# A tuned DeltaNet and feed-forward kernel: the second feed-forward product as seven half-width block products from the third chunk on

## Chip, cores, metric

One core of a Trainium2 chip. The metric is device time in microseconds. The kernel before has a median of 737.25 us over four runs (736.81 to 739.62).

## The reference, cut to what matters

```python
# attention: per batch and head a delta-rule recurrence over 768 tokens, 4 batches, 8 heads of 48
# then x: (3072, 384), w_in: (384, 2048), w_out: (2048, 384), alpha: (2048,)
h = x @ w_in
g = np.maximum(h, 0.0) + alpha * np.minimum(h, 0.0)
return (g @ w_out).astype(np.float32)
```

All of it is fp32. The kernel cuts the sequence into 12 chunks of 64 tokens x 4 batches = 256 tokens each.

## The kernel before

A chunk's feed-forward is two products: `ffn_in` (L639) and `ffn_out` (L669). Python generators emit both in small parts and `weave` mixes them with the attention steps, so that TensorE always has feed-forward matmuls to do while attention waits for VectorE and ScalarE. An attention *step* is half a chunk; steps 4 to 23 are woven so. Each engine is given its instructions in the order in which the program emits them.

```python
def ffn_in(c):
    for f in range(0, FT, 2):                       # 8 groups of 2 row tiles
        p_h = ps_ffn().rearrange(...)               # one of two PSUM banks
        for i in range(2):
            for t in range(KT):                     # KT = 3
                nc.tensor.matmul(p_h[:, i], w_in[...], xt[:, t], ...)      # 128x256, L639
        nc.scalar.activation(low, p_h, ACT.Relu, scale=-1.0)
        for i in range(2):
            nc.vector.scalar_tensor_tensor(out=g[:, i], in0=low[:, i], ..., in1=p_h[:, i], ...)

def ffn_out(c, together=False):                     # order: bp = 0, 1; f = 0..15
    nc.tensor.matmul(p_o[bp], gs[f // 2][:, f % 2, bp * 128 : (bp + 1) * 128],
                     w_out[:, f], ...)              # 128x384, L669: 32 matmuls
    if f == FT - 1:
        nc.scalar.copy(o_sb, p_o[bp])
        ...                                         # two stores of 64 rows

for n in range(NJ, N):                              # NJ = 4, N = 24
    gens = [(attention(n), SHARES), (placing(n + 1, (1, 2)), SHARES * PLACING)]
    ...                                             # VectorE's block elimination, 3 steps of 4
    if n < NJ + 2:
        gens.append((part(late, ...), ...))         # second product of the second chunk
    else:
        gens.append((part(tail, (IN_PARTS + OUT_PARTS) // 2), ...))   # 40 parts a step
    weave(*gens)
```

## Time and profile before

| what | before |
|---|---|
| median time, span of the profiled run | 737.25 us, 733.0 us |
| TensorE busy | 706.1 us, 96% |
| VectorE busy | 400.3 us, 55% |
| one chunk's second product, nothing woven in | 20.66 us, 64 records |
| step 5 | 14.9 us, VectorE busy 95% of it |

Busy shares say what is full on average; the chain of waits says which engine sets the end; the table by stage says how much room the others have, and where. The lines are in the prediction. A "record" is one matmul instruction in the trace: a full fp32 matmul of this program leaves two of them.

### The profile page before, as it was taken

Reading aid. Unit: us, or ns where it says so; the run is one execution under the profiler, and the core shown is the slowest. Engines: PE = TensorE matmul, PEld = TensorE weight load, DVE = VectorE, ACT = ScalarE, POOL = GpSimd, SP = SyncE. Lnnn points to the kernel's source line nnn. Section 1 sums busy time; section 2 is a strip of 40 time slices with the busy share of each in tenths; the row PEclk is TensorE's granted clock in tenths of the full one; section 3 lists DMA queues with packets and bytes.
Section 4 is the critical chain, followed back from the end, with each engine's and each line's share of the span. In section 5 each row is a group of like instructions: output and inputs, shape, how many; then the busy total and the mean of one; then the engine's idle time right before and its main releaser. Section 6 shows DMA issues by size and latency. Waiting matters only on the chain.

```text
span 733.0 us, 20599 instructions
## 1 busy us (share of the span) xinstructions
PE 706.1 (96%) x8993; PEld 516.9 (71%) x8993; DVE 400.3 (55%) x1015; ACT 257.9 (35%) x606; POOL 18.1 (2%) x72
## 2 busy tenths in 40 slices
PE   6999978799999999999999999999999999999997
PEld 5457766556678678678678678678687687686774
DVE  6976889896886247655257565157464042141120
ACT  4625666505444144144134134134033132221110
POOL 3000001000000000000000000000000000000000
PEclk9999999999999999999999999999999999999999
DMA  8815863212322122122111201201211220100000
GB/s 146 205 30 139 193 167 95 74 22 45 58 56 45 24 45 45 26 42 45 30 39 34 45 14 33 45 15 33 44 21 25 44 39 7 34 2 2 23 1 21
DMA packets 110187, 37.63 MB, mean 51 GB/s; under 512 B 103392, under 2 KB 106480, under 8 KB 110096
## 3 DMA queue, kind: packets, MB, share of 16 engines
q1 hardware_dynamic: 108512, 36.01, 23.2%
q8 instruction: 71, 1.16, 0.7%
q10 hardware_dynamic: 1584, 0.30, 0.2%
q14 instruction: 20, 0.16, 0.1%
HBM read 31.56 MB, written 4.72 MB: 49 GB/s over the span
## 4 chain that ended last, share of the span: by engine, by line
PE 81%; DVE 11%; ACT 4%; issue 1%; DMA 1%; SPq 0%; DVEq 0%
PE p_ffn L669 33%; PE p_ffn L639 27%; PE p_ffn L737 5%; PE p_big L569 3%; PE p_big L341 2%; PE p_big L374 2%; DVE g L650 2%; PE p_big L596 2%; PE p_big L583 2%; PE p_big L526 2%; PE p_big L541 1%; PE p_big L612 1%; DVE prod L452 1%; DVE block L458 1%; DVE w_out L212 1%
## 5 line engine op out<-in xcount | busy, mean ns | idle before, releaser
L639 PE MATMUL p_ffn<-xt,w_in 128*128 128x256 f32 x1152 | 268.8, 386 | 9.8 <-DVE g L650 4.8
L669 PE MATMUL p_ffn<-w_out,g 128*128 128x384 f32 x768 | 258.8, 490 | 2.4 <-DVE g L650 2.4
L639 PEld LDWEIGHTS p_ffn<-xt,w_in 128*128 128x128 f32 x1152 | 213.2, 190 | 43.1 <-ACT w_out L200 6.8
L669 PEld LDWEIGHTS p_ffn<-w_out,g 128*128 128x128 f32 x768 | 142.6, 190 | 93.1 <-issue 2.9
L650 DVE SCALAR_TENSOR_TENSOR g<-low,al_t,p_ffn 128x256 f32<-128x256 f32 x192 | 83.5, 476 | 113.0 <-ACT low L647 111.9
L647 ACT ACTIVATE low<-p_ffn 128x512 f32<-128x512 f32 x96 | 57.2, 596 | 113.1 <-PE p_ffn L639 87.8
L675 ACT COPY o_sb<-p_ffn 128x384 f32<-128x384 f32 x24 | 11.5, 479 | 182.7 <-PE p_ffn L669 182.7
L458 DVE TENSOR_TENSOR block<-block,prod 128x30 f32<-128x30 f32 (+9 forms) x180 | 59.7, 332 | 6.2
L452 DVE TENSOR_TENSOR prod<-block 128x30 f32<-128x30 f32 (+9 forms) x180 | 58.9, 327 | 4.0
L572 DVE TENSOR_TENSOR r<-v_raw,p_big 128x384 f32<-128x384 f32 x22 | 12.0, 551 | 79.6 <-PE p_big L569 79.6
L737 PE MATMUL p_ffn<-k_t,ident 128*128 128x512 f32 x82 | 38.0, 611 | 0.0
L603 DVE TENSOR_TENSOR y<-y,p_big 128x384 f32<-128x384 f32 x22 | 12.1, 548 | 40.5 <-PE p_big L596 40.5
L418 ACT COPY same<-right 32x256 f32<-32x256 f32 x40 | 16.1, 403 | 49.4 <-DVE right L383 49.1
L737 PEld LDWEIGHTS p_ffn<-k_t,ident 128*128 128x128 f32 x82 | 15.3, 195 | 16.6 <-issue 16.2
L492 ACT ACTIVATE diag<-inverse,which 64x128 f32<-64x128 f32 (+2 forms) x62 | 25.3, 411 | 1.0
L577 ACT COPY y<-p_big 128x384 f32<-128x384 f32 x22 | 10.5, 480 | 35.5 <-DVE r L572 35.5
L363 ACT COPY k_t<-p_big 128x512 f32<-128x512 f32 x24 | 13.9, 581 | 24.3 <-PE p_big L341 24.2
L328 DVE RECIPROCAL rec<-norm 128x8 f32<-128x8 f32 x24 | 4.8, 200 | 31.2 <-ACT norm L326 31.1
L596 PEld LDWEIGHTS p_big<-u,a_t 64*64 64x64 f32 x768 | 13.4, 134 | 11.2 <-issue 8.2
L492 ACT ACTIVATE inv<-inverse,which 128x256 f32<-128x256 f32 x43 | 20.6, 502 | 0.5
L363 ACT COPY q_t<-p_big 128x512 f32<-128x512 f32 x24 | 14.0, 588 | 16.5 <-PE p_big L341 16.5
L392 DVE TENSOR_TENSOR a_t<-p_big,minus 128x256 f32<-128x256 f32 x48 | 17.8, 415 | 3.2 <-PE p_big L374 3.2
(97 smaller groups left out, 638.7 us busy)
## 6 DMA issues: line engine op xcount, KB each, us to landing
w_out<-in_moe_w_in_dram SPq DMA_DIRECT2D x12, 512.0 KB, 5.5
qp<-in_q_dram SPq DMA_DIRECT2D x48, 96.0 KB, 3.0
v_raw<-in_v_dram SPq DMA_DIRECT2D x48, 96.0 KB, 2.9
kl<-in_k_dram SPq DMA_DIRECT2D x96, 48.0 KB, 2.4
out_dram<-o_sb SPq DMA_DIRECT2D x48, 96.0 KB, 2.2
space_out<-in_moe_w_out_dram SPq DMA_DIRECT2D x11, 384.0 KB, 4.4
ke<-in_k_dram SPq DMA_DIRECT2D x43, 96.0 KB, 3.5
w_out<-in_moe_w_out_dram SPq DMA_DIRECT2D x5, 384.0 KB, 3.3
```

The lines of the kernel that those rows point to most:

```text
L363: nc.scalar.copy(dst.rearrange("p g i -> p (g i)"), src)
L392: nc.vector.tensor_tensor(out=a_t[n_q][:, a * G : (a + 1) * G], in0=p[:, a, 1], in1=minus[:, None, :].to_broadcast([128, G, C]), op=ALU.mult,)
L452: nc.vector.tensor_tensor(out=prod, in0=r[:, 0:j, j : j + 1].to_broadcast([128, j, n]), in1=r[:, j : j + 1, j + 1 : HB].to_broadcast([128, ...
L458: nc.vector.tensor_tensor(out=r[:, 0:j, j + 1 : HB], in0=r[:, 0:j, j + 1 : HB], in1=prod, op=ALU.add)
L492: nc.scalar.mul(dst[n % NE][to or rows, a.start * G : a.stop * G, cols], src[m][rows, heads], which[rows, i : i + 1],)
L569: nc.tensor.matmul(p[half(t), a, w, g], x[n][dims(a), g, half(t)], state[bp][dims(a), t, g])
L596: nc.tensor.matmul(p[half(t), a, g], a_t[n][half(t ^ a), a * G + g], us[n][half(t ^ a), a, g])
L639: nc.tensor.matmul(p_h[:, i], w_in[:, t, (f + i) * 128 : (f + i + 1) * 128], xt[:, t], start=(t == 0), stop=(t == KT - 1),)
L647: nc.scalar.activation(low, p_h, ACT.Relu, scale=-1.0)
L650: nc.vector.scalar_tensor_tensor(out=g[:, i], in0=low[:, i], scalar=al_t[:, f + i : f + i + 1], in1=p_h[:, i], op0=ALU.mult, op1=ALU.add,)
L669: nc.tensor.matmul(p_o[bp], gs[f // 2][:, f % 2, bp * 128 : (bp + 1) * 128], w_out[:, f], start=(f == 0), stop=(f == FT - 1),)
L737: nc.tensor.matmul(p, ident, k_t[NJ - 1].rearrange("p g i -> p (g i)"))
```

## The change

The second product is a 2x2 block product: token halves by column halves, contracted over even and odd row tiles. Strassen's scheme (in the variant with fifteen sums) makes it of seven block products instead of eight. The intent is to take an eighth off the arithmetic of the largest term of TensorE's chain (L669, 33%) and to give the sums to VectorE, which had 45% of its time free. The core of the diff, cut:

```diff
+    def operand_sums(b):
+        for dst, x, y, op in (
+            (s1, a21, a22, ALU.add), (s2, s1, a11, ALU.subtract), (a21, a11, a21, ALU.subtract),
+            (s4, a12, s2, ALU.subtract),
+        ):
+            nc.vector.tensor_tensor(out=dst, in0=x, in1=y, op=op)      # 128x512
+            yield
+    def weight_sums(b, first, last):                # 128x768, four for each half b, once
...
     def ffn_in(c):
+                    if (i, t) == (0, KT - 1):
+                        next(later, None)           # at most one sum in each later group
+            if c >= FAST and f == FT // 2 - 2:
+                later = operand_sums(0)
...
+    def ffn_out_fast(c):
+        later = operand_sums(1)
+        def product(x, w):
+            p = ps_ffn()[:, 0 : DM // 2]
+            for i in range(FP):                     # 8 matmuls of 192 columns
+                nc.tensor.matmul(p, x(i), w(i), start=(i == 0), stop=(i == FP - 1))
+                if i % 2 == 1:
+                    next(later, None)
...
+        p = yield from product(operand(0, 0), weight(0, 0))
+        nc.scalar.copy(u[0], p)
+        p = yield from product(operand(1, 0), weight(1, 0))
+        add(o[0][:, left], u[0], p)
+        p = yield from product(sum_(1), w_sum_(1))  # the first that reads a sum
+        add(u[0], u[0], p)
...                                                 # four more products, adds on VectorE
-            gens.append((part(tail, (IN_PARTS + OUT_PARTS) // 2), (IN_PARTS + OUT_PARTS) // 2))
+            parts = IN_PARTS - 4 if n % 2 == 0 else FAST_PARTS + 4
+            gens.append((part(tail, parts), parts))
+        if n == NJ + 1:
+            gens.append((weight_sums(0, 0, 3), 3))
+        elif n == NJ + 2:
+            gens.append((chain(weight_sums(1, 0, 3), weight_sums(0, 3, 4)), 4))
+        elif n == NJ + 3:
+            gens.append((weight_sums(1, 3, 4), 1))
```

Besides: the activation is written in place, into one buffer for all chunks but the second (whose activation goes where the sums will be), the two PSUM banks are fixed by name, tokens are regrouped so that a chunk's halves are contiguous, and each half is stored in four pieces of 32 rows instead of two of 64.

More of the change, by code (lines that the diff above doesn't have):

```diff
@@ L78, in ps_one @@
         return ps_big()[:, 0]
+    ffn_banks = [psum.tile([128, 512], FP32, name=f"p_ffn{i}") for i in range(2)]
+    turn = [0]
     def ps_ffn():
-        return psum.tile([128, 512], FP32, name="p_ffn", tag="ffn", bufs=2)
+        turn[0] ^= 1
+        return ffn_banks[turn[0]]
     def half(i):
@@ L621, in to_ffn @@
             xts[c] = work.tile([128, KT, TOK], FP32, name="xt", tag="xt", bufs=NXT)
-        p = ps_one()[:, 0:DM].rearrange("p (t i) -> p t i", t=KT)
+        p = ps_one()[:, 0:DM]
         y = ys[n].rearrange("p h d -> p (h d)")
         for t in range(KT):
-            nc.tensor.transpose(p[:, t], y[:, t * 128 : (t + 1) * 128], ident)
-        nc.scalar.copy(xts[c][:, :, bp * 128 : (bp + 1) * 128], p)
-    gss = {}
+            nc.tensor.transpose(p[:, t * 128 : (t + 1) * 128], y[:, t * 128 : (t + 1) * 128], ident)
@@ new lines, in to_ffn, with act_of @@
+        nc.scalar.copy(
+            xts[c].rearrange("p k (u b t i) -> p b k u t i", u=2, b=NB, t=2)[:, bp],
+            p.rearrange("p (k t u i) -> p k u t i", k=KT, t=2, u=2),
+        )
+    gss = {}
+    FP = FT // 2
+    act = const.tile([128, FP, 2, TOK], FP32, name="act")
+    sums = const.tile([128, FP, 3, 128], FP32, name="sums")
+    more = const.tile([128, FP // 2, 3, DM // 2], FP32, name="more")
+    FAST = 2
+    def act_of(c, i):
+        if c != 1:
+            return act[:, i]
+        flat = sums.rearrange("p i s e -> p (i s e)")
+        if i >= 6:
+            i, flat = i - 6, more.rearrange("p i s e -> p (i s e)")
+        return flat[:, i * 512 : (i + 1) * 512].rearrange("p (f i) -> p f i", f=2)
@@ new lines, in operand_sums @@
+    def operand_sums(b):
+        x = act[:, 4 * b : 4 * b + 4].rearrange("p i f (u e) -> p i f u e", u=2)
+        a11, a12, a21, a22 = x[:, :, 0, 0], x[:, :, 1, 0], x[:, :, 0, 1], x[:, :, 1, 1]
+        s1, s2, s4 = (sums[:, 4 * b : 4 * b + 4, i] for i in range(3))
+        for dst, x, y, op in (
[4 more added lines that the diff above has]
+            yield
@@ new lines, with w_sum @@
+    w_half = w_out.rearrange("p (i f) (v e) -> p i f v e", f=2, v=2)
+    def w_sum(i, x):
+        if x == 3:
+            return w_half[:, i, 0, 1]
+        n = 3 * (DM // 2)
+        if i < FP // 2:
+            flat = space_out.rearrange("p s e -> p (s e)").bitcast(FP32)
+        else:
+            i, flat = i - FP // 2, more.rearrange("p i s e -> p (i s e)")
+        return flat[:, i * n + x * (DM // 2) : i * n + (x + 1) * (DM // 2)]
+    summed = []
+    def weight_sums(b, first, last):
+        n = 3 * (DM // 2)
+        if b == 0:
+            flat = space_out.rearrange("p s e -> p (s e)").bitcast(FP32)
+        else:
+            flat = more.rearrange("p i s e -> p (i s e)")
+        t1, t2, t3 = (
+            flat.rearrange("p (i x e) -> p x i e", x=3, e=DM // 2)[:, x] for x in range(3)
+        )
+        own = w_half[:, 4 * b : 4 * b + 4]
+        b11, b12, b21, b22 = own[:, :, 0, 0], own[:, :, 0, 1], own[:, :, 1, 0], own[:, :, 1, 1]
+        for dst, x, y in (
+            (t1, b12, b11), (t2, b22, t1), (t3, b22, b12), (b12, b21, t2)
+        )[first:last]:
+            nc.vector.tensor_tensor(out=dst, in0=x, in1=y, op=ALU.subtract)
+            summed.append(b)
+            yield
@@ L633, in ffn_in @@
         gs = gss[c] = []
+        later = iter(())
         for f in range(0, FT, 2):
@@ L642, in ffn_in @@
                     )
+                    if (i, t) == (0, KT - 1):
+                        next(later, None)
                     if (i, t) != (1, KT - 1):
                         yield
-            low = work.tile([128, 2, TOK], FP32, name="low")
-            nc.scalar.activation(low, p_h, ACT.Relu, scale=-1.0)
-            g = work.tile([128, 2, TOK], FP32, name="g", bufs=FT)
+            g = act_of(c, f // 2)
+            nc.scalar.activation(g, p_h, ACT.Relu, scale=-1.0)
             for i in range(2):
                 nc.vector.scalar_tensor_tensor(
-                    out=g[:, i], in0=low[:, i], scalar=al_t[:, f + i : f + i + 1], in1=p_h[:, i],
+                    out=g[:, i], in0=g[:, i], scalar=al_t[:, f + i : f + i + 1], in1=p_h[:, i],
                     op0=ALU.mult, op1=ALU.add,
@@ L654, in ffn_in, with store @@
             gs.append(g)
+            if c >= FAST and f == FT // 2 - 2:
+                later = operand_sums(0)
             yield
+        for _ in later:
+            pass
+    def store(c, u, o_sb):
+        for b in range(B):
+            tok = b * S + c * C + 32 * u
+            nc.sync.dma_start(out=out[tok : tok + 32, :], in_=o_sb[32 * b : 32 * b + 32])
     def ffn_out(c, together=False):
@@ L661, in ffn_out @@
         if together:
-            order = [(bp, f) for f in range(FT) for bp in range(NB)]
+            order = [(u, f) for f in range(FT) for u in range(2)]
         else:
-            order = [(bp, f) for bp in range(NB) for f in range(FT)]
-        for bp, f in order:
+            order = [(u, f) for u in range(2) for f in range(FT)]
+        for u, f in order:
             assert len(out_done) > f
             if f == 0:
-                p_o[bp] = ps_ffn()[:, 0:DM]
+                p_o[u] = ps_ffn()[:, 0:DM]
             nc.tensor.matmul(
-                p_o[bp], gs[f // 2][:, f % 2, bp * 128 : (bp + 1) * 128], w_out[:, f],
+                p_o[u], gs[f // 2][:, f % 2, u * 128 : (u + 1) * 128], w_out[:, f],
                 start=(f == 0), stop=(f == FT - 1),
@@ L674, in ffn_out, with operand, sum_, weight @@
                 o_sb = work.tile([128, DM], FP32, name="o_sb")
-                nc.scalar.copy(o_sb, p_o[bp])
-                for t in range(2):
-                    tok = (2 * bp + t) * S + c * C
-                    nc.sync.dma_start(out=out[tok : tok + C, :], in_=o_sb[half(t)])
+                nc.scalar.copy(o_sb, p_o[u])
+                store(c, u, o_sb)
             yield
+    def ffn_out_fast(c):
+        gss.pop(c)
+        later = operand_sums(1)
+        o = [work.tile([128, DM], FP32, name="o_sb") for _ in range(2)]
+        left, right_ = slice(0, DM // 2), slice(DM // 2, DM)
+        u = [work.tile([128, DM // 2], FP32, name=f"u{i}", bufs=1) for i in (2, 3)]
+        def product(x, w):
[4 more added lines that the diff above has]
+                    next(later, None)
+                    if i < FP - 1:
+                        yield
+            return p
+        def operand(f, u):
+            return lambda i: act[:, i, f, u * 128 : (u + 1) * 128]
+        def sum_(x):
+            return lambda i: sums[:, i, x]
+        def weight(f, v):
+            return lambda i: w_half[:, i, f, v]
+        def w_sum_(x):
+            return lambda i: w_sum(i, x)
+        def add(to, x, p):
+            nc.vector.tensor_tensor(out=to, in0=x, in1=p, op=ALU.add)
+        p = yield from product(operand(0, 0), weight(0, 0))
+        nc.scalar.copy(u[0], p)
+        yield
+        p = yield from product(operand(1, 0), weight(1, 0))
+        add(o[0][:, left], u[0], p)
+        yield
+        for _ in later:
+            assert False
+        assert summed.count(0) == summed.count(1) == 4
+        p = yield from product(sum_(1), w_sum_(1))
+        add(u[0], u[0], p)
+        yield
+        p = yield from product(lambda i: act[:, i, 0, 128:256], w_sum_(2))
+        add(u[1], u[0], p)
+        yield
+        p = yield from product(sum_(0), w_sum_(0))
+        add(o[0][:, right_], u[0], p)
+        add(o[1][:, right_], u[1], p)
+        yield
+        p = yield from product(sum_(2), weight(1, 1))
+        add(o[0][:, right_], o[0][:, right_], p)
+        store(c, 0, o[0])
+        yield
+        p = yield from product(operand(1, 1), w_sum_(3))
+        add(o[1][:, left], u[1], p)
+        store(c, 1, o[1])
+        yield
@@ L681 @@
     in_done, out_done = [], []
-    IN_PARTS, OUT_PARTS = FT * KT, NB * FT
+    IN_PARTS, OUT_PARTS, FAST_PARTS = FT * KT, NB * FT, 7 * FP // 2
     def part(gen, n):
@@ L912, in feed_forward @@
             yield from ffn_in(c)
-            yield from ffn_out(c)
+            yield from ffn_out_fast(c)
     tail = feed_forward()
```

## The prediction

> **What bounds the kernel now.** I read the page first: busy shares of each engine, the forty slices, the chain that ended last, the costliest groups.
>
> ```profile
> PE 706.1 (96%) x8993; PEld 516.9 (71%) x8993; DVE 400.3 (55%) x1015; ACT 257.9 (35%) x606; POOL 18.1 (2%) x72
> ...
> PE   6999978799999999999999999999999999999997
> ...
> DVE  6976889896886247655257565157464042141120
> ...
> PE 81%; DVE 11%; ACT 4%; issue 1%; DMA 1%; SPq 0%; DVEq 0%
> PE p_ffn L669 33%; PE p_ffn L639 27%; PE p_ffn L737 5%; PE p_big L569 3%; PE p_big L341 2%; PE p_big L374 2%; DVE g L650 2%; PE p_big L596 2%; PE p_big L583 2%; PE p_big L526 2%; PE p_big L541 1%; PE p_big L612 1%; DVE prod L452 1%; DVE block L458 1%; DVE w_out L212 1%
> ...
> L639 PE MATMUL p_ffn<-xt,w_in 128*128 128x256 f32 x1152 | 268.8, 386 | 9.8 <-DVE g L650 4.8
> L669 PE MATMUL p_ffn<-w_out,g 128*128 128x384 f32 x768 | 258.8, 490 | 2.4 <-DVE g L650 2.4
> L639 PEld LDWEIGHTS p_ffn<-xt,w_in 128*128 128x128 f32 x1152 | 213.2, 190 | 43.1 <-ACT w_out L200 6.8
> L669 PEld LDWEIGHTS p_ffn<-w_out,g 128*128 128x128 f32 x768 | 142.6, 190 | 93.1 <-issue 2.9
> ```
>
> TensorE is busy in nine tenths or more of nearly every slice after the eighth, and the two feed-forward products are 60% of the chain. VectorE has about half its time free on average, but its row swings between 1 and 8 tenths, so it must be read by stage. The program issues 384 matmuls at L669 (12 chunks x 32); the trace has 768, so one fp32 matmul is two records. The 190 ns of a weight load will matter below.
>
> The price of a record comes from the end of the chain of waits, where nothing is woven in:
>
> ```profile
> 699.97 8.20 PE p_ffn L639 x38
> 708.17 20.66 PE p_ffn L669 x64
> ```
>
> Columns: start, microseconds, work. 20.66/64 = 323 ns a record for 384 moving columns; 8.20/38 = 216 ns for 256. That is two array cycles at 2.4 GHz per column plus some 3 ns (768/2.4 + 3; 512/2.4 + 3). One chunk's second product is 20.66 us of pure TensorE time.
>
> Then VectorE by step. A step is one attention iteration with its share of feed-forward; I cut at the starts of the subtraction at L572. These are steps 8 to 11, the third to sixth in which the changed stretch runs:
>
> ```profile
> core 0: us, PE busy (x) PEld busy (x) DVE busy (x) ACT busy (x) POOL busy (x), PEclk, DMA share, GB/s
> 195.00:210.00 15.00, 15.00 (x328) 10.60 (x327) 14.24 (x40) 7.13 (x19) 0.56 (x2) 1.00 0.45 82
> 263.40:287.60 24.20, 23.99 (x399) 20.57 (x392) 18.61 (x51) 10.22 (x24) 0.51 (x2) 1.00 0.22 43
> 287.60:318.10 30.50, 30.50 (x387) 20.55 (x379) 17.70 (x46) 8.70 (x22) 0.51 (x2) 1.00 0.18 34
> 318.10:341.90 23.80, 23.80 (x399) 20.62 (x395) 16.61 (x42) 10.22 (x24) 0.41 (x2) 1.00 0.23 43
> 341.90:372.40 30.50, 30.50 (x386) 20.55 (x379) 6.80 (x16) 8.69 (x22) 0.41 (x2) 1.00 0.18 34
> ```
>
> The reader should see two things: TensorE never waits (step 5, the first row, even holds with VectorE at 95%), and VectorE is at 77%, 58%, 70% and 22%, because the block elimination runs in three steps of four.
>
> **What the Trainium skill says.** "TensorE: Matmul & The Clock Gate", section "LDWEIGHTS (loading the stationary operand)": a load costs its columns over 1.2 GHz, 107 ns for 128 columns. The trace shows 190 ns of record but agrees on the occupancy:
>
> ```profile
> 364.55 0.95 PEld L669 LDWEIGHTS p_ffn<-w_out,g 128*128 128x128 f32 x4
> ...
> 364.65 1.13 PE L669 MATMUL p_ffn<-w_out,g 128*128 128x384 f32 x3
> ```
>
> The first matmul behind a fresh load starts 0.10 us after that load starts. Same page, section "Back-to-back issue gap": warm, N/2.4 + 2.5 ns per pass; the trace agrees if a record is two passes over its columns. "VectorE: DVE Perf Modes", section "The TRN2 errata": an fp32 tensor_tensor takes (N+151)/0.96 ns; the trace's 384-element ones take about 550 (formula 557). "Perfetto Trace Analysis", section "Optimizing Scalar/DVE operations": half of the fixed latency overlaps the next instruction. The trace agrees:
>
> ```profile
> 198.98 0.55 DVE L587 TENSOR_TENSOR u<-p_big,wgt 128x384 f32<-128x384 f32 x1
> 199.44 0.41 DVE L383 TENSOR_TENSOR same<-p_big,wgt 128x256 f32<-128x256 f32 x1
> 199.77 0.41 DVE L383 TENSOR_TENSOR right<-p_big,wgt 128x256 f32<-128x256 f32 x1
> ```
>
> Starts are 0.46 apart behind 384 elements and 0.33 behind 256, so VectorE is occupied for about 65 ns + 1.02 ns an element.
>
> **The change, part by part.** Removed per chunk from the third on: 32 matmuls of 384 columns, 64 records, 20.66 us. Added: seven products of 8 matmuls with 192 columns, 112 records. Estimate of one: 2 x 192/2.4 + 2.5 = 162.5 ns, so 18.2 us. The gain is 2.46 us a chunk, x 10 chunks = 24.6 us, all on TensorE, which sets the end. One eighth of the arithmetic goes, and the per-record 2.5 ns takes little back. The weight loads rise from 64 to 112 a chunk, one every 162 ns; at 108 ns of occupancy they stay hidden.
>
> Added on VectorE per chunk: eight operand sums of 128x512, by the spacing above 0.59 us, some 0.62 with waits on each other, 5.0 us; seven additions of 128x192 from PSUM, about 0.3 us each, 2.0 us. So 7 us a chunk, 70 us in all. Once: eight weight differences of 128x768, 0.85 us each, 6.8 us, in steps 5 to 7. ScalarE loses two copies of 0.48 us a chunk and gets one smaller. The activation written in place of a separate buffer, the two fixed PSUM banks and the regrouped token order move no work; the stores double in number at half the size.
>
> Parts are shifted too: even steps carry 44 first-product matmuls instead of 40, odd steps 4 and the whole fast product.
>
> Even elimination step (8): VectorE 18.6 + 0.5 (more first product) + 2.5 (first half of the sums) = 21.6 us in 24.2 + 8 x 0.216 = 25.9, 83%. Odd one (9): 17.7 - 0.5 + 2.5 + 2.0 = 21.7 in 30.5 - 1.7 - 2.5 = 26.3, 83%. So on average VectorE fits. But it takes orders strictly in sequence and the sums come bunched: four in the second half of an even step, four in the first product of the next. In the first product of the layer a bank must be cleared by ScalarE (0.60) and VectorE (0.87) within one group's 2.6 us, which leaves under 1 us of lag; a fast product's bank tolerates about 2 us.
>
> What I take off for it, as judgement from those rows:
> - step 5 has 14.2 of 15.0 us used and gets three weight differences, 2.6 us: 1.9 lost.
> - step 6 gets four more and the first sums: 0.8.
> - steps 8, 12, 16: the second half goes to about 100% of VectorE: 0.9 each, 2.7.
> - steps 9, 13, 17: 0.3 each, 0.9; steps 10, 14, 18: 0.2 each, 0.6.
> - the end: four stores where two took 1.11 us to issue; the last addition is shorter than the copy it replaces: 0.8.
>
> Sum 7.7. Net 24.6 - 7.7 = 16.9 us, so 737.4 - 16.9 = 720.5.
>
> **The rivals.** First: the weight load binds. If a 128-column load really held the array's loader 190 ns, a record could not come more often than that, 112 x 190 = 21.3 us a chunk, and the change would lose 0.6 us a chunk: about 743 with nothing else. For it: the 190 ns records, longer than 162. Against: the 0.10 us between load and matmul. I give it one in twelve.
>
> Second: VectorE becomes the bound in the elimination steps, or each product waits for its sums. For it: 83% on average with bunching, and strict order. Against: step 5 ran at 95% with TensorE at 15.00 of 15.00. If the lag costs 1.5 us in each of the nine elimination steps from 8 on, plus steps 5 and 6 and the end as above, 17 us of the gain go and the time is about 730.
>
> Third: everything hides and only the end and step 5 cost: about 715. This is what the undisturbed steps of before speak for.
>
> Fourth: buffers. All chunks now share one activation buffer, where there were sixteen pieces for two chunks. The next chunk's first product writes a piece only after 2.6 us of matmuls that themselves stand behind the last fast product, so I expect no wait; but the sums are overwritten in place while neighbours are read, and if such neighbours are made to wait for each other, 1 us a chunk would go: about 730.
>
> **Range and chances.** The ceiling of gain (712.8) is out of reach by the end and step 5, so the low end is 714.5. Rivals two and four reach 730 only if they hold throughout; half of either gives 726. I take 714.5 to 728. The 2% line is 722.7, so my number lies only 2 us inside it: faster 0.67, the same 0.31, slower 0.02.
>
> **What would show it.** Record spacing of the fast products, from the undisturbed last chunk: 112 records in 18.2 us; 21 us means the load rival. The group of second-product matmuls should lose 10 x 64 = 640 records of 384 columns and gain 1120 of 192. VectorE's busy time should rise by 70 to 80 us, its share in steps 8 and 9 to 80-88%. Waits of the feed-forward matmuls on VectorE should sum to some 7 us; much more, with busy slices below 9 between the tenth and the thirtieth, means rival two or four, told apart by which VectorE line releases them. I am wrong if the spacing is not 162 ns, or if the sums cost more than 0.62 us each.

## The result, and the profile after

The changed kernel takes 713.87 us (712.95 to 715.02, 4 runs) beside 737.25 of before. The ratio is 0.9677, 95% interval 0.9652 to 0.9703: 3.2% faster. A ratio is the mean time of one kernel's fast runs over that of the other's of the same rounds, so it is not quite the ratio of the medians. The time lies 6.6 us under the predicted 720.5 and 0.6 us under the low end of the range.

The page of the changed kernel, the same rows as shown of before. L709 is now the first product, L772 the fast one, L792 its additions; its row names split by which buffer holds the operands.

```profile
PE 683.1 (96%) x9473; PEld 580.0 (81%) x9473; DVE 476.5 (67%) x1173; ACT 251.2 (35%) x596; POOL 18.5 (3%) x72
...
PE   5999987889999999999999999999999999999997
...
DVE  6976889886898738868638968538967436245151
...
L772 PE MATMUL p_ffn<-w_out,act 128*128 128x192 f32 x480 | 83.7, 328 | 0.0
L772 PEld LDWEIGHTS p_ffn<-w_out,act 128*128 128x128 f32 x480 | 78.6, 190 | 0.9
...
L792 DVE TENSOR_TENSOR o_sb<-u,p_ffn 128x192 f32<-128x192 f32 x40 | 13.2, 351 | 42.4 <-PE p_ffn L772 36.1
```

VectorE gained 76.2 us of work (476.5 - 400.3; 70 to 80 were predicted) and TensorE is as full as before: the column of idle time ahead of the fast product's matmuls says 0.0. VectorE's own idle time ahead of its additions is spent waiting for TensorE, not the reverse.

The end of the chain of waits, where only the last chunk runs:

```profile
669.10 20.72 PE p_ffn L709 x96
689.82 18.21 PE p_ffn L772 x112
708.03 0.02 issue
708.06 0.35 DVE o_sb L792
```

18.21/112 = 162.6 ns a record against 162.5 estimated; the second product went from 20.66 to 18.21 us a chunk. From the end of the last addition (before: the last copy) to the end of the span, four stores now take about as long as two did: 712.3 - 708.4 = 3.9 us, before 733.0 - 729.3 = 3.7.

Steps 5 to 11 of the changed kernel, cut at the starts of the same VectorE subtraction, columns as before:

```profile
197.00:214.10 17.10, 15.73 (x330) 11.17 (x329) 16.45 (x43) 7.13 (x19) 0.56 (x2) 1.00 0.45 84
214.10:239.10 25.00, 23.84 (x364) 19.90 (x364) 21.68 (x52) 10.59 (x25) 1.01 (x2) 1.00 0.21 40
239.10:265.50 26.40, 26.40 (x439) 25.35 (x433) 12.25 (x29) 7.44 (x20) 0.41 (x2) 1.00 0.20 40
265.50:291.70 26.20, 26.20 (x416) 22.59 (x409) 21.18 (x56) 10.71 (x25) 0.41 (x2) 1.00 0.20 39
291.70:317.60 25.90, 25.69 (x404) 24.70 (x405) 21.23 (x57) 7.44 (x20) 0.50 (x2) 1.00 0.21 40
317.60:343.00 25.40, 25.40 (x400) 22.01 (x395) 19.44 (x47) 10.71 (x25) 0.41 (x2) 1.00 0.21 41
343.00:369.40 26.40, 26.40 (x436) 25.35 (x433) 11.36 (x27) 7.44 (x20) 0.41 (x2) 1.00 0.20 39
```

The reader should see that TensorE has no gap in these rows from step 7 on beyond 0.2 us, with VectorE at 81%, 82% and 77% in the elimination steps 8, 9 and 10. All that TensorE waits for from step 8 to the end (waiter and releaser, us in total, times, longest; "issue" is time in which the profile shows nothing that was waited for):

```profile
PE p_big L530 <- issue: 0.9, 1, 0.9
PE p_ffn L709 <- issue: 0.2, 1, 0.2
```

VectorE is not among the releasers. The even steps are longer than before by the matmuls that were moved into them; step 5 got none and still became longer, from 14.9 to 17.1 us, with TensorE busy for 15.73 of 17.10; step 6 has a gap of 1.2 us. In step 5 the chain of waits runs through VectorE and shows who is new there (L696 are the weight differences):

```profile
198.28 0.87 DVE space_out L696
...
204.36 0.87 DVE space_out L696
...
210.43 0.87 DVE space_out L696
```

Three times 0.87 us in a step in which VectorE had been busy for 95%.

A sum over the profiles: from the start of step 6 to the end before took 733.0 - 210.0 = 523.0 us, after 712.3 - 214.1 = 498.2. That is 24.8 us less, beside the 24.6 that the array's arithmetic promises. That the two agree so closely is in part luck: the 498.2 hold the gap of step 6 and a wait of 0.9 us in step 15. move_w below, without the first, takes 708.5 - 212.2 = 496.3 us from step 6 on, 26.7 less than before; what gives the 2 us beyond the arithmetic stays open. Step 5 takes 2.2 back. The rest of the difference between the two profiles is ahead of step 4, which starts at 180.0 us before and 181.9 after; in the profiles of the experiments below, with the changed kernel's program up to there, it starts anywhere from 180.0 to 184.6, so this is scatter and nothing that I read a cause into.

### The profile page after: what moved, and what is told of

Same layout as the page of the kernel before. It is cut to its first block, busy times and chain, and to the rows that moved or that the text cites.

```text
span 712.3 us, 21783 instructions
## 1 busy us (share of the span) xinstructions
PE 683.1 (96%) x9473; PEld 580.0 (81%) x9473; DVE 476.5 (67%) x1173; ACT 251.2 (35%) x596; POOL 18.5 (3%) x72
## 3 DMA queue, kind: packets, MB, share of 16 engines
q1 hardware_dynamic: 109280, 36.01, 23.4%
## 4 chain that ended last, share of the span: by engine, by line
PE 81%; DVE 12%; ACT 5%; issue 1%; DMA 1%; SPq 0%; DVEq 0%
PE p_ffn L709 29%; PE p_ffn L772 26%; PE p_ffn L878 5%; PE p_ffn L750 4%; PE p_big L378 3%; PE p_big L573 3%; PE p_big L345 3%; PE p_big L600 2%; PE p_big L587 2%; PE p_big L530 2%; PE p_big L545 1%; PE p_big L616 1%; DVE prod L456 1%; DVE block L462 1%; DVE act L721 1%
## 5 line engine op out<-in xcount | busy, mean ns | idle before, releaser
L709 PE MATMUL p_ffn<-xt,w_in 128*128 128x256 f32 x1152 | 269.7, 387 | 9.5 <-DVE sums L721 3.2
L709 PEld LDWEIGHTS p_ffn<-xt,w_in 128*128 128x128 f32 x1152 | 213.9, 191 | 42.8 <-ACT w_out L204 6.8
L721 DVE SCALAR_TENSOR_TENSOR act<-act,al_t,p_ffn 128x256 f32<-128x256 f32 x176 | 76.4, 476 | 72.3 <-ACT act L719 71.4
L719 ACT ACTIVATE act<-p_ffn 128x512 f32<-128x512 f32 x88 | 52.3, 594 | 117.1 <-PE p_ffn L709 116.9
L772 PE MATMUL p_ffn<-w_out,act 128*128 128x192 f32 x480 | 83.7, 328 | 0.0
L772 PEld LDWEIGHTS p_ffn<-w_out,act 128*128 128x128 f32 x480 | 78.6, 190 | 0.9
L792 DVE TENSOR_TENSOR o_sb<-u,p_ffn 128x192 f32<-128x192 f32 x40 | 13.2, 351 | 42.4 <-PE p_ffn L772 36.1
L878 PEld LDWEIGHTS p_ffn<-k_t,ident 128*128 128x128 f32 x82 | 15.6, 199 | 17.1 <-issue 16.7
L772 PE MATMUL p_ffn<-space_out,sums 128*128 128x192 f32 x160 | 29.3, 326 | 0.0
L772 PE MATMUL p_ffn<-more,sums 128*128 128x192 f32 x160 | 29.3, 326 | 0.0
L772 PE MATMUL p_ffn<-w_out,sums 128*128 128x192 f32 x160 | 27.7, 326 | 0.0
L772 PEld LDWEIGHTS p_ffn<-space_out,sums 128*128 128x128 f32 x160 | 26.5, 190 | 0.0
L772 PEld LDWEIGHTS p_ffn<-more,sums 128*128 128x128 f32 x160 | 26.5, 190 | 0.0
L792 DVE TENSOR_TENSOR u<-u,p_ffn 128x192 f32<-128x192 f32 x20 | 7.0, 352 | 28.9 <-PE p_ffn L772 28.7
L772 PEld LDWEIGHTS p_ffn<-w_out,sums 128*128 128x128 f32 x160 | 25.8, 190 | 0.0
```

The lines of the kernel that those rows point to most:

```text
L709: nc.tensor.matmul(p_h[:, i], w_in[:, t, (f + i) * 128 : (f + i + 1) * 128], xt[:, t], start=(t == 0), stop=(t == KT - 1),)
L719: nc.scalar.activation(g, p_h, ACT.Relu, scale=-1.0)
L721: nc.vector.scalar_tensor_tensor(out=g[:, i], in0=g[:, i], scalar=al_t[:, f + i : f + i + 1], in1=p_h[:, i], op0=ALU.mult, op1=ALU.add,)
L772: nc.tensor.matmul(p, x(i), w(i), start=(i == 0), stop=(i == FP - 1))
L878: nc.tensor.matmul(p, ident, k_t[NJ - 1].rearrange("p g i -> p (g i)"))
```

## The experiments

Eight kernels, each one edit away from the changed kernel. "Theory B" is the prediction's reason for taking 5.0 us off for steps 6 to 18: bunched sums make the products wait. "Theory A" came from the profile: from step 7 on VectorE's new work is hidden whole, and step 5 alone costs.

| run | median us | ratio to before | 95% interval |
|---|---|---|---|
| the changed kernel | 713.87 | 0.9677 | 0.9652 to 0.9703 |
| no_sums (wrong) | 713.63 | 0.9678 | 0.9655 to 0.9701 |
| sums_x2 | 722.29 | 0.9796 | 0.9773 to 0.9819 |
| sums_x3 | 764.22 | 1.0381 | 1.0353 to 1.0409 |
| bunched | 716.51 | 0.9726 | 0.9700 to 0.9752 |
| move_w | 711.39 | 0.9646 | 0.9621 to 0.9670 |
| plain_out | 736.83 | 1.0007 | 0.9989 to 1.0024 |
| narrow | 782.70 | 1.0628 | 1.0584 to 1.0673 |
| w_pool | 719.94 | 0.9778 | 0.9749 to 0.9806 |

Step lengths in us, read from the traces at the same cuts; steps 8, 9, 12 and 13 have elimination, 11 and 19 do not, and "last" runs from step 23 to the end of the span:

| kernel | 5 | 6 | 8 | 9 | 11 | 12 | 13 | 19 | last |
|---|---|---|---|---|---|---|---|---|---|
| changed | 17.1 | 25.1 | 26.2 | 26.0 | 26.3 | 26.2 | 25.6 | 25.4 | 65.2 |
| no_sums | 17.1 | 25.0 | 25.7 | 26.1 | 26.3 | 25.7 | 26.1 | 25.4 | 65.4 |
| sums_x2 | 17.1 | 25.6 | 26.8 | 27.9 | 26.4 | 26.8 | 27.9 | 25.4 | 65.2 |
| sums_x3 | 17.1 | 27.7 | 28.6 | 34.0 | 27.7 | 28.6 | 33.2 | 27.0 | 71.2 |
| bunched | 17.1 | 25.1 | 25.7 | 27.5 | 26.3 | 25.7 | 27.5 | 25.4 | 65.2 |
| move_w | 14.9 | 24.0 | 26.2 | 25.6 | 26.3 | 26.2 | 25.6 | 25.4 | 65.2 |

### no_sums: the eighty operand sums left out

```diff
-            nc.vector.tensor_tensor(out=dst, in0=x, in1=y, op=op)
             yield
```

> The changed kernel with the eighty operand sums of VectorE left out (a wrong result on purpose). Theory A, the array alone sets the steps from 7 on and VectorE is hidden there: within 1 us of the changed kernel's 713.9. Theory B, my prediction's, bunched sums stall the first product's banks: the 5 us that I took off for steps 6 to 18 come back, 709 or less. VectorE busy falls by some 54 us in both.

713.63 us, with a wrong result (relative error 1.6) and VectorE's busy time down from 476.5 to 430.9 us. (That is 45.6 us and not the 54 expected: the sums' records add up to 54.6, but overlap their neighbours.) The sums cost nothing that can be measured. None of the five runs (711.2 to 715.8) reaches theory B's 709: it falls for the change as it stands. The step table shows it finer: steps 8 and 9 together are 51.8 us without the sums and 52.1 with them, 12 and 13 together 51.8 in both.

### sums_x2 and sums_x3: every sum issued two and three times

```diff
             nc.vector.tensor_tensor(out=dst, in0=x, in1=y, op=op)
+            if dst is a21:
+                dst, x, y = s2, s1, a11            # the sum in place can't be repeated; s2 can
+            for _ in range(1):                     # 2 for sums_x3
+                nc.vector.tensor_tensor(out=dst, in0=x, in1=y,
+                                        op=ALU.add if dst is s1 else ALU.subtract)
             yield
```

> Every operand sum issued twice (result unchanged): some 50 us more of VectorE, about 2.4 us more in each step. Theory A: the elimination steps go from 81% to about 90% of VectorE, still under the 95% at which step 5 ran before without a wait: 714 to 716. Theory B: stalls double or more, 719 or above.

> Every operand sum issued three times: the elimination steps reach 26 us of VectorE work in 25.4 to 26.2 us, so VectorE binds in the fullest of them. Theory A: only what overflows is lost, some 0.5 to 1.5 us in each of six to nine steps, 718 to 726. Theory B: 726 or above.

Both miss theory A's numbers and lie where theory B put them. Doubling costs about 8 us (722.29), not up to 2, and tripling 50 (764.22), not up to 12. So the room was smaller than the average share of VectorE suggests: the doubled steps 9 and 13 have it at 88% and lose 1.9 and 2.3 us against the changed kernel, which stood at 82 and 83%. And theory B's mechanism exists. The tripled kernel's last chunk, where no attention is left and VectorE is not full on average, shows it plainly. These are TensorE's records of the third product, in two halves, and of the first half of the fourth, with the wait before them in brackets (L667 are the repeats of the sums, L796 the additions):

```profile
740.33 1.46 PE L776 MATMUL p_ffn<-space_out,sums 128*128 128x192 f32 x8
743.91 1.57 PE L776 MATMUL p_ffn<-more,sums 128*128 128x192 f32 x8 [2.12 <-DVE sums L667]
746.38 1.57 PE L776 MATMUL p_ffn<-space_out,act 128*128 128x192 f32 x8 [0.90 <-DVE o_sb L796]
```

The third product, the first that reads a sum, starts in time, on sums made during `ffn_in`. Its second half waits 2.12 us, until the ninth of the twelve sums that stand in the first product is done. The fourth product then waits 0.90 us for the bank of the second: VectorE's addition that empties it stands behind all twelve, which take 8.4 us (737.6 to 746.0). The step table agrees: in steps 11 and 19, without elimination, tripling costs 1.3 and 1.6 us and doubling (eight sums in that place, 5.5 us in step 11) nothing. There the tripled sums delay the attention too: of its waits in steps 11 and 19, 1.08 us each are an attention product (L600) waiting for a VectorE result behind the sums, 0.41 and 0.90 us the third product's.

### bunched: all eight sums ahead of the first fast product

```diff
-                later = operand_sums(0)                  # in ffn_in
+                later = iter(())
...
-        later = operand_sums(1)                          # in ffn_out_fast
+        for b in range(2):
+            for _ in operand_sums(b):
+                pass
+        later = iter(())
```

> All eight operand sums of a chunk stand ahead of the first fast product instead of four in the layer before and four spread over that product. Theory A': the first product's bank is emptied by ScalarE and the sums are first read by the third product, so VectorE may lag by two products (5.3 us bare): no loss where there is no elimination, some 2 us in each of steps 9, 13 and 17 as in the doubled sums, 0.5 us back in steps 8 and 12: 717 to 721. Rival, my prediction's tolerance of one product: about 2.5 us lost in every chunk, 735 or more.

716.51 us, a bit under the range that I expected, far from the rival's 735. Nothing is lost where there is no elimination (steps 11, 19, last) and 1.5 and 1.9 us in steps 9 and 13. From step 8 on, TensorE waits for VectorE three times, once in each of steps 9, 13 and 17. First the total of these waits, then the second half of the third product and the wait in step 9:

```profile
PE p_ffn L775 <- DVE o_sb L795: 3.7, 3, 1.3
```

```profile
300.44 1.46 PE L775 MATMUL p_ffn<-more,sums 128*128 128x192 f32 x8
...
304.79 1.57 PE L775 MATMUL p_ffn<-space_out,act 128*128 128x192 f32 x8 [1.32 <-DVE o_sb L795]
```

The third product does not wait for its sums; the fourth waits for the bank of the second, because VectorE comes to the addition that empties it only after the lump and the elimination work behind it. Without elimination a lump of 5.1 us on VectorE is free: ScalarE empties the first product's bank, the third product is the first to need a sum, and the fourth the first to need a bank that VectorE empties behind the lump.

### move_w: the weight differences out of step 5

```diff
-        if n == NJ + 1:
+        if n == NJ + 2:
             gens.append((weight_sums(0, 0, 3), 3))
-        elif n == NJ + 2:
-            gens.append((chain(weight_sums(1, 0, 3), weight_sums(0, 3, 4)), 4))
         elif n == NJ + 3:
-            gens.append((weight_sums(1, 3, 4), 1))
+            gens.append((chain(weight_sums(1, 0, 3), weight_sums(0, 3, 4), weight_sums(1, 3, 4)), 20))
```

(The 20 makes the five of them come in the first quarter of step 7, before the third product.)

> The three weight differences of step 5 move to step 6 and the others to step 7, which has no elimination. Theory A: step 5, the only one that VectorE lengthened (15.0 to 17.1 us), goes back to 15 us; 1.5 to 2.1 us faster than the changed kernel, about 712. Rival: step 5 is longer for another reason (the moved parts or the activation layout), and the time stays at 714.

711.39 us, 2.5 under the changed kernel and the fastest. Steps 5 and 6 of its profile:

```profile
197.30:212.20 14.90, 14.90 (x327) 10.53 (x326) 14.14 (x40) 7.13 (x19) 0.56 (x2) 1.00 0.47 87
212.20:236.20 24.00, 24.00 (x371) 20.70 (x370) 21.18 (x51) 10.61 (x25) 0.41 (x2) 1.00 0.24 47
```

Step 5 is back to 14.90 us, and the gap in step 6 went too: TensorE is busy for 24.00 of 24.00. The 95% intervals of the two kernels' ratios overlap, so the step lengths, not the medians alone, carry this.

### plain_out: the plain second product, all side changes kept

```diff
-            yield from ffn_out_fast(c)
+            yield from ffn_out(c)
...
-            parts = IN_PARTS - 4 if n % 2 == 0 else FAST_PARTS + 4
+            parts = (IN_PARTS + OUT_PARTS) // 2
```

(and neither operand sums nor weight differences)

> The changed kernel with the plain second product for all chunks and the old even split of parts; the token order, the activation in place in one buffer, the two fixed banks and the halved stores stay. Theory A, the gain is the array's alone: the kernel before, 736 to 739. Rival, the side changes have a share of 2 us or more: 734 or less, or 740 or more.

736.83 us, ratio 1.0007: the in-place activation, the single buffer, the fixed banks, the token order and the doubled stores move nothing. The gain belongs to the seven products with their uneven split of parts over the steps. The split was not tried alone; in the profile of before TensorE waits for only 0.7 us in all from step 4 on, so there was next to nothing for it to gain.

### narrow: the same products in halves of 96 columns

```diff
-            for i in range(FP):
-                nc.tensor.matmul(p, x(i), w(i), start=(i == 0), stop=(i == FP - 1))
-                if i % 2 == 1:
+            e = DM // 4
+            for v in range(2):
+                at = slice(v * e, v * e + e)
+                for i in range(FP):
+                    nc.tensor.matmul(p[:, at], x(i), w(i)[:, at], start=(i == 0), stop=(i == FP - 1))
+                    if i % 4 == 3:
```

> Each product in two halves of 96 columns: 224 records a chunk. If a 128-column weight load holds the loader 108 ns, records come every 108 to 109 ns, 24.3 us a chunk instead of 18.2, and the time is about 774. If only the moving columns count (82.5 ns), 18.5 us a chunk and about 717. If it were 190 ns, 42.6 us a chunk and over 950.

782.70 us, some 9 above what I expected. The last chunk:

```profile
752.88 25.00 PE p_ffn L775 x224
```

25.00/224 = 111.6 ns a record where the moving columns alone would take 82.5. So here something other than the moving columns sets the pace. The weight load fits, at 112 ns and not at the 190 ns that its record shows; no run changes the load alone, so that it is the load and no other fixed cost of a record is argued, not shown. The sign and the mechanism of the second outcome are ruled out, as is the third; the first was 3 ns short per record.

### w_pool: the weight differences on GpSimd

```diff
-            nc.vector.tensor_tensor(out=dst, in0=x, in1=y, op=ALU.subtract)
+            nc.gpsimd.tensor_tensor(out=dst, in0=x, in1=y, op=ALU.subtract)
             summed.append(b)
```

> The eight weight differences on GpSimd, which has 3% of its time used, at their old places. Theory A: VectorE gets its 95% of step 5 back and the step returns to about 15 us, 711 to 712. Rival: GpSimd slows VectorE when both work, or its differences end too late for the third product: 714 or more.

719.94 us: the rival, and stronger than I had put it. GpSimd, which has nothing else to do, starts them early, in step 4. First its row, then VectorE's at the same time:

```profile
193.85 1.81 POOL L696 TENSOR_TENSOR space_out<-w_out 128x768 f32<-128x768 f32 x1 [0.29 <-DMA out_dram<-o_sb]
195.74 1.83 POOL L696 TENSOR_TENSOR space_out<-w_out,space_out 128x768 f32<-128x768 f32 x1
197.53 1.95 POOL L696 TENSOR_TENSOR space_out<-w_out 128x768 f32<-128x768 f32 x1
```

```profile
193.53 0.39 DVE L456 TENSOR_TENSOR prod<-block 128x220 f32<-128x220 f32 x1
193.95 1.95 DVE L462 TENSOR_TENSOR block<-block,prod 128x220 f32<-128x220 f32 x1
195.94 1.88 DVE L456 TENSOR_TENSOR prod<-block 128x228 f32<-128x228 f32 x1
197.85 1.88 DVE L462 TENSOR_TENSOR block<-block,prod 128x228 f32<-128x228 f32 x1
```

Elimination operations that take 0.39 us take 1.9 while a GpSimd operation runs, each ending some 0.25 us after one of them. The Trainium skill has this: "SBUF — State Buffer", section "Who interferes with whom", says that "a DVE instruction with two SBUF inputs contends with a GpSimd instruction that reads SBUF" and that the ports they share are "an exclusive lock". The trace agrees. Steps 4 and 5 take 19.6 and 20.9 us instead of 15.1 and 17.1.

## Why the prediction was right or wrong

- **The array's term was right.** Predicted 162.5 ns a record, 18.2 us a chunk, 24.6 us in all; measured 162.6 ns, 18.21 us, and 24.8 us from step 6 on (the last in part by luck, as said above). The direction was right with it, and plain_out shows that the side changes did not contribute. The formula behind 162.5, from section "Back-to-back issue gap" of "TensorE: Matmul & The Clock Gate", is given there for an isolated matmul, and the section says that a stream with weight loads is spaced otherwise, which the prediction left out; in this kernel's streams the formula holds for 192, 256 and 384 columns (162.6, 216 and 323 ns).
- **The load rival was rightly set aside,** though on thin evidence: the 0.10 us between load and matmul is seen behind the attention's transposes (L341, L625), while behind its smaller matmuls the two records start together (both at 188.32 in one place). narrow shows how near the rival was: 112 ns against 162, and halving the columns a second time meets it.
- **VectorE's added work was right in size** (76 us for the predicted 77), and so was its share in steps 8 and 9 (81 and 82% for 83).
- **Step 5 was right:** 1.9 us predicted, 2.2 measured; move_w takes it back.
- **What failed is the deduction for bunched sums:** 4.2 us for steps 8 to 18 (2.7 + 0.9 + 0.6). The prediction expected TensorE to wait some 7 us for VectorE; from step 4 on the profile has 2.6 us of such waits, all in steps 5 and 6 and none from step 8 on, and no_sums is only 0.2 us faster by its median and 0.4 in steps 8 and 9. The 0.8 for the stores at the end failed too: they cost 0.2. (The gap in step 6 is real, 1.2 us for 0.8, but it is the weight differences': no_sums leaves it, move_w closes it.) The premise was that a fast product's bank tolerates about 2 us of VectorE's lag. I counted from the end of a product to the next use of its bank, and forgot that the lump of four sums, 2.6 us in the last chunk, stands in the first product, whose bank ScalarE empties. The first reader of one of its sums is the third product, no sooner than two products or 5.2 us after the first began, and the first bank that VectorE empties behind it is needed by the fourth, after three products or 7.8 us; with attention woven in both times are longer.
- **The measured edges of that tolerance:** eight sums (5.1 us in bunched, 5.5 in sums_x2) are free without elimination and cost 1.3 to 2.3 us in steps 9, 13 and 17, twelve (8.4) cost 1.3 to 1.7 even in steps without it, and 3.0 in the last chunk. In `ffn_in`'s groups the lag allowed is 2.6 - 0.60 - 0.87 = 1.1 us by the prediction's own figures ("under 1"), but the program puts at most one sum of 0.6 us into each group, and I charged the average of a half step instead.
- **The range** took its low end from the ceiling, 712.8 by 24.6 us, plus step 5. With that and no other deduction the sum is 737.4 - 24.6 + 1.9 = 714.7, so the low end of 714.5 had left next to no room for rival three being right, and none for the run-to-run scatter of about 2 us. Rival three, everything hides but the end and step 5, is what came. (Half of rival two gives 712.8 + 3.5 + 6.75 = 723 by the prediction's own sums, not 726.)
- **The other way round, theory A was too generous.** A second set of sums is free only in steps without elimination; where VectorE reaches 88% of a step it already costs 2 us.

What stays open: the runs' medians give a gain of 23.4 us, the profiles 20.7, since the profiled run of before was among its fastest (734.82 us) and steps began at different times ahead of step 4. I did not look for the cause of that scatter.

## What to carry to other kernels

To price work moved to an engine that has room, don't deduct for bunching by the average share: find the first instruction that needs a result of the bunch, and the first that needs a buffer or a result which the receiving engine handles behind the bunch; add up what the busy engine can do until each, and compare it with the bunch. Charge only the stages where the receiving engine was already nearly full, as a once-only 2.6 us in a step at 95% cost 2.2 us here, and 46 us of sums spread over steps at 83% and less cost under 1. And an algorithm that shrinks a matmul's moving side is worth its eighth only while a record stays longer than the floor that narrow met, 112 ns here.

## What the Trainium skill lacked or had wrong

- "TensorE: Matmul & The Clock Gate": it gives 107 ns for loading 128 columns and doesn't say that the record of such a load is far longer. Here the record is 190 ns, loads were started 112 ns apart in narrow's stream (25.00 us for 224), and a stream at 162.6 ns a record was not slowed by them.
- No page says how a true fp32 matmul shows in a trace. Here one is two records, each with its own weight load and 0.84 ns per moving column: 162.6, 216 and 323 ns for 192, 256 and 384 columns.
- No page that I read says how much lag of an evacuating engine a pair of PSUM banks absorbs. Here, with 2.6 us of matmuls a bank and the first bank emptied by another engine, lumps of 5.1 and 5.5 us were free where VectorE had little else to do, and lumps of 8.4 us cost 1.3 to 3.0 us there.
